# Sending the first 256 tokens ahead, spreading sums of v by engines, two rings of PSUM banks and another sequence, in a long-short attention and feed-forward kernel

## The chip, the core and the metric

The kernel runs on one core of one Trainium2 chip. A core has a matrix engine (TensorE, in profiles PE, with its weight loads as PEld), a vector engine (VectorE, DVE), a scalar engine (ScalarE, ACT), a general engine (GpSimd, POOL) and a sync engine (SyncE, SP), which here issues all DMAs. Each runs its own queue of instructions in order and waits for the others by semaphores. SBUF is the core's working memory with 128 partitions, PSUM the memory that PE writes its products to, in banks. The metric is the device time in microseconds (us); lower is better.

## The reference

Attention over 4 batches, 8 heads, 768 positions and 64 dimensions, with keys near the query and a summary of each block of 32 keys, and then a feed-forward net with softplus:

```python
k_sum = k.reshape(B, H, nb, block, D).max(axis=3)          # block = 32
v_sum = v.reshape(B, H, nb, block, D).mean(axis=3)
scores_l = scale * np.matmul(q, k.transpose(0, 1, 3, 2))
mask_l = np.abs(pos[:, None] - pos[None, :]) < window       # window = 16
scores_s = scale * np.einsum('bhsd,bhnd->bhsn', q, k_sum) + np.log(block)
scores_all = np.concatenate([np.where(mask_l, scores_l, -1e9), scores_s], axis=-1)
a = np.exp(scores_all - max); a = a / (sum(a) + 1e-09)
x = a @ concatenate([v, v_sum])       # then (3072 tokens, 512)
h = x @ w_in                          # 512 x 2048
g = np.maximum(h, 0.0) + np.log1p(np.exp(-np.abs(h)))       # softplus
out = g @ w_out                       # 2048 x 512
```

All is fp32.

## The kernel before

**Precision.** PE's fast 32-bit format keeps fewer bits than fp32, so each large product is made from two parts of each factor: x = xh + xl, w = high + low, and three matmuls, xh·high, xl·high, xh·low. So the weights too must be taken apart on the chip before use.

**Units of work.** The 3072 tokens are 12 chunks of 256. Chunks are handled in groups: [0,1], [2], [3,4], and so on to [11]. The feed-forward net is cut into 16 tiles of d_ff, f = 0 to 15, of 128 each. A step f of group x is written fx.f: a product (`product`, L823, into a bank `ph`), softplus twice on ACT (rounded into `gh`, L843, and exact, in place, L847), the rest `gl` = exact - rounded on DVE (L851), and the matmuls with w_out into banks `po` (L860). The phases are group 0 with f0 to f10, group 1 with f0 to f10, group 0 with f11 to f15, group 1 with f11 to f15, and from group 2 on all 16 steps in one.

**Weights.** Weight tile w0 to w15 (one of w_in and one of w_out, for all 128 of its d_ff) is loaded once (`raw`, L738 and L741) and stays in SBUF. Its chain is: magnitude (DVE L754 or ACT L757), clamp (DVE L761), shift (DVE L765), sign (DVE L769), tail (ACT L775 or DVE L778), the sum of both (`t<-t,raw`, POOL L783), `high` (ACT or DVE, L787) and `low` (DVE or POOL, L794). The work tile `t` comes from a ring of two. w0 and w1 go in two halves of 512 columns, the others in one of 1024.

**Attention** of a chunk goes by pairs of heads, four to a chunk, written ax.i.hp for chunk i of group x: scores on PE (L601), mask and maximum on DVE (L614), exponentials on ACT (L622), their inverse sums on DVE (L629, L630), normalisation on DVE or POOL (L635), a transpose, values on PE (L692, into `xo`), then xh on ACT (L708) and xl on DVE (L712). For group 0 PE transposes (`pt`, L648, copied to `pT` by ACT, L652); for the others DVE transposes blocks (L661) and DMAs through DRAM do the rest. The block sums of keys are a reduction on DVE (L329). Those of v are for the first batch matmuls with ones (`vt`, L407) and a copy by ACT (`vn`, L420), for the others additions on DVE or POOL (L357 to L362). In group 0 the class `FirstPlaces` loads q and v of both chunks at once (L542, L550) and puts the sums of v beside the values by four DMAs that repeat each row for eight windows (`load_sums`, L555).

**Order.** The program is first recorded as some 1600 tasks, each with an engine and in some cases a second one. Then `issue` runs them in the order of a stored list of numbers, `SEQUENCE`; a letter behind a number picks the other engine. So the queue of each engine is fixed by hand before it starts, and a task that isn't ready holds up all that stand behind it in its engine's queue. PSUM banks: two of `ph` (shared with `vt` and later `xo`), one tile of two banks for scores, four of `po` (shared with `pt` and `xo` in group 0).

Of the kernel before, what the change touches and what calls it, by code (L numbers as in the profile page):

```python
# [152 lines left out]
171a 130 109 199 94 172 40 200 110 111 173 41 112 42 174 387 175 239 113 95 197 176 121 114 123 122 115 124 198
177 219 125 220 181a 178 309 209 126 182 185 318 127 201a 183 388 310 184 240 394 202 311 210 186 319 312 408
205 313 249 203 325 187 204 320 592 390 321 188 391 225 279 314 206 322 221a 315 395 316 594 250 317 207a 323
396 208 222 331 223 224 241a 326 397 324 398a 415 399 226 327 245 329 328 400 229 332 242 230 227 330 269 243
389 333 228 337 280 215 392 244 211a 334 246 335 416 338 343 212 213 339 247 214 336 248 344 345 341 417 340 216
574 401 346 393 342 595 347 591 217a 218 348 255 578 418 575 593 419 349 402 403 231a 404 289 235 232 233 355
350 234 579 236 351 352 353 576 356 290 420 357 600a 405 237a 421 270 238 603 406 358 251a 354 407 361 577a 252
580 422 253 367 362 409 254 413 412 604 256 363 425 423 359 368 411 275 424 364 410 257a 369 360 258 605 365  # L160
581a 584 414 373 588 618 259 295 606 370 366 374 585a 371 375 582 426 589 376 299 260 372 427 428 378 377 607
429 381 382a 583 383 435 300 430 431 619 432 380 436 271 437 379 438 433 272 434 273 586 441 620 274 596 617 447
442 608 276 621 443 439 448 444 609 449 265 440 450 453 277a 305 590 278a 459 454 455 456 445 587 384 446 261
451 626a 385 452 460 262 386 461 457 598 285 263 629 264 465 643 462 266 644 630 601 471 466 648a 645 467 610
458 468 472 463 267a 473 631 474 464 291 469 470 268 477 292 483 293 478 632 294 651 475 479 633a 666 484 667
485 476 281a 296 480 481 486 634 489 635 670a 282 482 297 602 498 283 612 490 284 613 665 298 491 487 499 492
286 500 652 488 301a 506 501 287a 653 302 673 288 502 794 597 303 493 797 304 494 796 507 795 512 599 495a 306
793 496a 508 611 497 509 503 654 307 655a 504 518 513 656 308a 514 515 657 674 505 524 532 519 536 802 520 675
521 614 805 636 622 510 637 625 676 638 677a 639 511 624 525 678 623 516 627 806 628 526 615 517 820 821 527 807
# [4 lines left out]
693 694 699 702 834 850 835 851 862 707 855 804 871 836 800 837 700 708 703 705 709 704 710 852a 706 713 856a  # L174
# [40 lines left out]
def kernel(  # L215
# [32 lines left out]
    NU = 4  # L248
# [18 lines left out]
    def bank(shape, name):  # L267
        return buffer(shape, F32, name, "ph", 2, psum, True)
# [255 lines left out]
    class FirstPlaces:  # L524


        def __init__(self, hp, sums, own, sp):
# [4 lines left out]
            def q(g):  # L532
                return own[g]()[:, :n_c * CH]
# [478 lines left out]
```

## Time and profile before

| what | us |
|---|---|
| median of 3 runs | 628.37 (627.63 to 628.79) |
| the profiled execution, its own time | 630.34 |
| its span in the trace | 628.5 |
| PE busy in the span | 611.5 (97%) |
| ACT busy | 311.7 (50%) |
| DVE busy | 277.5 (44%) |
| POOL busy | 83.2 (13%) |

The span is what the trace covers, from the first to the last instruction; the program's time has 1.84 us more around it. PE's busy time counts matmuls; its weight loads lie beside them. In lists of rows "start, duration, engine, line, operation, output<-inputs, shapes" a bracket behind a row tells how long the engine stood idle before it and for whom. In rows of groups the bar separates the count from the busy time, the mean in ns and the idle time before.

### The profile page before, as it was taken

The numbers are of one execution on the slowest core, as the hardware profiler recorded it, in microseconds if no ns is written. First come the engines' busy times: TensorE is split into PE (matmuls) and PEld (weight loads), VectorE is DVE, ScalarE is ACT, GpSimd is POOL, SyncE is SP. The second block draws the span as 40 slices with busy tenths as digits, with TensorE's granted clock in tenths as the row PEclk, the third lists the DMA queues.
The fourth block names the chain that finished last, engine by engine and source line by source line (L and its number), as shares of the span: only waits on it lengthen the run. The fifth ranks groups of instructions, "written<-read, shape, count | busy, mean of one in ns | idle before, by whom it ended". The sixth has DMA issues, their size and how long they took to land.

```text
span 628.5 us, 11315 instructions
## 1 busy us (share of the span) xinstructions
PE 611.5 (97%) x4348; PEld 505.5 (80%) x4348; DVE 277.5 (44%) x757; ACT 311.7 (50%) x752; POOL 83.2 (13%) x74
## 2 busy tenths in 40 slices
PE   4889999999999999999999999999999999999997
PEld 4478888888888888888888888888888888888996
DVE  5978988679644443212451444432411111341111
ACT  1789988479652554316472435462622222553222
POOL 5324341434310202101000030000000000000000
PEclk9799999999999999999999999999999999999999
DMA  8779678933767861241344553543300400311000
GB/s 292 234 244 347 217 190 242 291 92 113 231 199 212 236 181 63 86 139 43 135 152 131 176 141 107 153 144 110 100 0 1 141 0 2 108 66 68 34 1 33
DMA packets 84453, 85.72 MB, mean 136 GB/s; under 512 B 24528, under 2 KB 70192, under 8 KB 84400
## 3 DMA queue, kind: packets, MB, share of 16 engines
q1 hardware_dynamic: 84400, 85.01, 44.0%
q8 instruction: 34, 0.56, 0.4%
q14 instruction: 19, 0.16, 0.1%
HBM read 64.23 MB, written 18.35 MB: 131 GB/s over the span
## 4 chain that ended last, share of the span: by engine, by line
PE 95%; DMA 1%; issue 1%; POOL 1%; SPq 1%; ACT 0%; DVE 0%; POOLq 0%; DVEq 0%
PE po L860 42%; PE ph L823 42%; PE sc L601 4%; PE xo L692 4%; DMA first<-v_hp_dram 1%; PE vt L407 1%; PE warm L934 1%; POOL added L296 0%; SPq L555 0%; PE pt L648 0%; DVE sp L614 0%; ACT sp L622 0%; SPq L738 0%; SPq L741 0%; ACT vn L420 0%
## 5 line engine op out<-in xcount | busy, mean ns | idle before, releaser
L823 PE MATMUL ph<-xh,w 128*128 128x512 f32 (+1 forms) x896 | 257.6, 360 | 0.0
L860 PE MATMUL po<-w,gh 128*128 128x512 f32 x768 | 201.1, 392 | 0.0
L823 PEld LDWEIGHTS ph<-xh,w 128*128 128x128 f32 x896 | 161.7, 189 | 27.2 <-issue 0.5
L851 DVE TENSOR_TENSOR gl<-ph,gh 128x512 fp32r<-128x512 f32 (+1 forms) x112 | 68.1, 611 | 222.4 <-ACT ph L847 203.8
L860 PEld LDWEIGHTS po<-w,gh 128*128 128x128 f32 x768 | 142.1, 188 | 29.5 <-issue 0.5
L823 PE MATMUL ph<-xl,w 128*128 128x512 f32 (+1 forms) x448 | 160.8, 359 | 0.0
L843 ACT ACTIVATE gh<-ph 128x512 fp32r<-128x512 f32 (+1 forms) x112 | 60.2, 537 | 196.0 <-PE ph L823 169.4
L860 PE MATMUL po<-w,gl 128*128 128x512 f32 x384 | 113.7, 393 | 0.0
L823 PEld LDWEIGHTS ph<-xl,w 128*128 128x128 f32 x448 | 84.5, 189 | 13.1
L860 PEld LDWEIGHTS po<-w,gl 128*128 128x128 f32 x384 | 71.0, 188 | 15.5 <-issue 1.0
L622 ACT ACTIVATE sp<-sp,nm 128x120 f32<-128x120 f32 x192 | 73.1, 383 | 2.5 <-DVE nm L614 2.3
L847 ACT ACTIVATE ph<-ph 128x512 f32<-128x512 f32 (+1 forms) x112 | 59.4, 532 | 0.0
L783 POOL TENSOR_TENSOR t<-t,raw 128x1024 int32<-128x1024 int32 (+1 forms) x18 | 43.5, 2421 | 81.7 <-DVE t L769 24.9
L614 DVE CUSTOM_DVE_ANT_0 sp<-sc,added 128x120 f32<-128x120 f32 x192 | 40.7, 278 | 15.2 <-PE sc L601 15.0
L843 ACT ACT_TABLE_LOAD x24 | 30.8, 1283 | 33.5 <-PE ph L823 31.7
L622 ACT ACTIVATION_READ_ACCUMULATOR sp<-sp,nm 128x1 f32 x192 | 36.1, 188 | 0.0
L712 DVE TENSOR_TENSOR xl<-xo,xh 128x512 fp32r<-128x512 f32 x24 | 16.5, 687 | 39.1 <-ACT xh L708 39.1
L708 ACT CAST xh<-xo 128x512 fp32r<-128x512 f32 x24 | 14.1, 590 | 39.2 <-PE xo L692 39.2
L661 DVE STREAM_TRANSPOSE tb<-sp 128x1024 f32<-128x1024 f32 x20 | 24.8, 1240 | 2.3 <-POOL sp L635 2.0
L692 PEld LDWEIGHTS xo<-pT,v 120*64 120x64 f32 x640 | 20.3, 138 | 6.7 <-issue 6.2
L635 POOL TENSOR_TENSOR sp<-sp,ss 128x960 f32<-128x960 f32 x7 | 12.5, 1793 | 98.3 <-DVE ss L630 75.9
L622 ACT ACT_TABLE_LOAD x18 | 23.1, 1283 | 4.8 <-DVE nm L614 4.5
(64 smaller groups left out, 389.7 us busy)
## 6 DMA issues: line engine op xcount, KB each, us to landing
squares<-tb SPq DMA_DIRECT2D x20, 512.0 KB
pT<-squares SPq DMA_DIRECT2D x80, 128.0 KB
raw<-w_in_dram SPq DMA_DIRECT2D x16, 512.0 KB
raw<-w_out_dram SPq DMA_DIRECT2D x16, 512.0 KB
kf<-kT_dram SPq DMA_DIRECT2D x16, 384.0 KB
out_dram<-ob SPq DMA_DIRECT2D x11, 512.0 KB
q<-qT_dram SPq DMA_DIRECT2D x20, 256.0 KB
st<-v_hp_dram SPq DMA_DIRECT2D x12, 384.0 KB
```

Source lines behind the costliest of these rows:

```text
L601: nc.tensor.matmul(unit(g * NU + h * NPAIR + i)[r * QW:(r + 1) * QW, k0:k1], lhsT=q[rows, w * QW:(w + 1) * QW], rhs=k[rows], start=True, s ...
L614: nc.vector.tensor_tensor_reduce(out=sp()[:, n], in0=unit(n), in1=added()[:, kinds.index((lows[w], lows[w + 1]))], scale=-SCALE, scalar=FL ...
L622: nc.scalar.activation(sp()[:, n], sp()[:, n], AF.Exp, bias=nm()[:, n:n + 1], scale=-1.0, accum_out=ss()[:, n:n + 1],)
L661: nc.vector.transpose(out=tb().rearrange("p k (u q) -> p u k q", q=SQ), in_=tiles.sp().rearrange("p u (k q) -> p u k q", q=SQ),)
L692: nc.tensor.matmul(xo()[h * D:(h + 1) * D, g * CH + w * QW:g * CH + (w + 1) * QW], lhsT=tiles.v(g)[:, w, h * D:(h + 1) * D], rhs=queries(g ...
L712: nc.vector.tensor_sub(out=of_x(xl), in0=of_bank(), in1=of_x(xh).bitcast(F32))
L783: nc.gpsimd.tensor_tensor(a, a, word(0, I32), op=ALU.add)
L823: nc.tensor.matmul(ph()[:, :n_x], lhsT=w1()[:, i1, part, cc * P:(cc + 1) * P], rhs=a()[:, cc, :n_x], start=cc == 0 and i == 0, stop=cc == ...
L843: nc.scalar.activation(gh()[:, :n_x], ph()[:, :n_x], AF.Softplus)
L847: nc.scalar.activation(ph()[:, :n_x], ph()[:, :n_x], AF.Softplus)
L851: nc.vector.tensor_sub(out=gl()[:, :n_x], in0=ph()[:, :n_x], in1=gh()[:, :n_x].bitcast(F32),)
L860: nc.tensor.matmul(po[t](), lhsT=a()[:, t * P:(t + 1) * P], rhs=w2()[:, i2, part], start=f == f0 and i == 0, stop=f == f1 - 1 and i == 2,)
```

## The change

Six things change.

1. q and v of group 0 are loaded by chunk and pair of heads (`load_q`, `load_v`), where q and most of v came for both chunks at once. Eight loads of q stand for four, 18 of v for 14.
2. The four DMAs `load_sums` go; eight copies `spread` (24 x 512 elements each) on POOL, DVE or ACT come. The sequence puts five on POOL, one on DVE and two on ACT.
3. Attention of group 0 is declared chunk by chunk, where it was head pair by head pair. Product, softplus, rest and second matmuls of group 0 are made for each chunk of 256 tokens apart in f0, f1 and f2 (`AHEAD = 3`), so that chunk 0 can go through three steps before chunk 1 is there.
4. The ring of four `po` banks becomes two rings of two, `po0` and `po1`, filled in turn by chunk (`half`, `turns`); `pt` takes the ring of its chunk, `xo` of group 0 the second.
5. The copy of `pt` to SBUF and that of xh in group 0 may run on DVE as well.
6. The sequence is another, with other choices of engine. Up to w15: ten magnitudes of 1024 columns more on DVE and ten fewer on ACT, six `low` more on POOL and six fewer on DVE, five `high` fewer on DVE, two tails more on DVE, five normalisations more on POOL and three fewer on DVE.

The diff, cut to its core:

```diff
 SEQUENCE = """
-2 133 43 160 45 64 68 47 1 0 96 134 3 49 4 138a 5 51 135 44 6 7 97 161a 136 8 100 137 9 142 46 10 11 165a 53 12
...
+    def half(h, shape, name):
+        return buffer(shape, F32, name, f"po{h}", 2, psum)
...
-    SPLIT = NF // 2
+    AHEAD = 3
...
     for x, f0, f1 in phases:
+        turns[x, f0] = turn
+        turn = (turn + len(groups[x])) % 2
...
-                def load_q(g=g):
-                    src = qT[0, groups[0][0]:groups[0][-1] + 1, :, hp + g].rearrange("j p c -> p j c")
-                    nc.sync.dma_start(out=q(g).rearrange("p (j c) -> p j c", c=CH), in_=src)
...
-                def load_sums(g=g):
-                    src = sums.first(hp + g).rearrange("n (o c) -> n o c", o=1)
-                    nc.sync.dma_start(out=v(g)[KW:], in_=src.broadcast_to([NB, n_w, P]))
...
+                    def load_q(g=g, i=i, j=j):
+                        nc.sync.dma_start(out=q(g, i), in_=qT[0, j, :, hp + g])
...
+                    def spread(copy, g=g, w0=w0):
+                        src = sums.first(hp + g).rearrange("n (o c) -> n o c", o=1)
+                        copy(out=v(g)[KW:, w0:w0 + NWIN], in_=src.broadcast_to([NB, NWIN, P]))
+                    tiles.v_keys.append((own[g], "sums", i))
+                    order.add(
+                        POOL, pool(NWIN * P), lambda f=spread: f(nc.gpsimd.tensor_copy), [sums.first_v], [tiles.v_keys[-1]],
+                        ways=[
+                            Way(DVE, dve(NWIN * P), lambda f=spread: f(nc.vector.tensor_copy), port=True),
+                            Way(ACT, act(NWIN * P), lambda f=spread: f(nc.scalar.copy)),
+                        ],
+                    )
...
-                pt = buffer([P, NU * P], F32, "pt", "po", NT, psum)
+                pt = half(i, [P, NU * P], "pt")
...
-        xo = buffer([P, NG * CH], F32, "xo", "po", NT, psum) if by_pe else bank([P, NG * CH], "xo")
+        xo = half(1, [P, NG * CH], "xo") if by_pe else bank([P, NG * CH], "xo")
...
-        po = [buffer([P, DM], F32, "po", "po", NT, psum) for _ in range(n_t)]
+        h0 = turns[x, f0]
+        po = [half((h0 + t // 2) % 2, [P, DM], "po") for t in range(n_t)]
...
+            split = x == 0 and f < AHEAD
+            for part in [(i,) for i in range(size)] if split else [tuple(range(size))]:
+                ph = bank([P, CT], "ph")
+                cols = slice(part[0] * CH, (part[-1] + 1) * CH)
...
-        for i, tiles in enumerate(places.tiles):
-            n = hp // NG * len(places.tiles) + i
-            attention(0, i, hp, tiles, T0 - 1.5 - 4.0 * (NHP // NG * len(places.tiles) - 1 - n), True)
+        places.append(FirstPlaces(hp, sums, own, scratch(12 + hp // NG, "sp0")))
+    for i in range(len(groups[0])):
+        for hp in range(0, NHP, NG):
+            attention(0, i, hp, places[hp // NG].tiles[i], T0, True)
```

The new lines of the operations are: magnitude L771, clamp L778, shift L782, sign L786, tail L795 on DVE, POOL's sum L800, `high` L804, `low` L811, rest L876, transpose L675, normalisation L646, spread L564.

**First place: DVE's queue between two rests of group 0, where weight tiles w6 to w9 are made.** Before, between the rests of f2 and f3 (`t_771` is the work tile of w7, `t_832` that of w9; the `gl` are the rests):

```order
L851 TENSOR_TENSOR gl_889<-ph_737,gh_834 128x512
L761 TENSOR_SCALAR t_832<-t_832 128x1024
L765 TENSOR_SCALAR t_832<-t_832 128x1024
L794 TENSOR_TENSOR w_899<-t_771,w_899 128x2x512
L769 SCALAR_TENSOR_TENSOR t_832<-raw_587,t_832 128x1024
L851 TENSOR_TENSOR gl_930<-ph_817,gh_895 128x512
```

And now, between the rests of f3 and f4 (`t_972` is the work tile of w9, `t_990` that of w6, `tb_979` a transposed tile of chunk 2):

```order
L876 TENSOR_TENSOR gl_974<-ph_927,gh_940 128x512
L778 TENSOR_SCALAR t_972<-t_972 128x1024
L675 STREAM_TRANSPOSE tb_979<-sp_389 128x8x4x32
L782 TENSOR_SCALAR t_972<-t_972 128x1024
L786 SCALAR_TENSOR_TENSOR t_972<-raw_863,t_972 128x1024
L778 TENSOR_SCALAR t_990<-t_990 128x1024
L782 TENSOR_SCALAR t_990<-t_990 128x1024
L786 SCALAR_TENSOR_TENSOR t_990<-raw_877,t_990 128x1024
L876 TENSOR_TENSOR gl_1030<-ph_948,gh_977 128x512
```

Between the two rests stood four operations on weights; now there are six and a transpose, and the `low` of w9 stands behind the second rest.

**Second place: POOL's queue at the start, after the constants.** Before (`t<-t,raw` is the sum of a weight tile, `w<-t,w` its `low`):

```order
L783 TENSOR_TENSOR t_152<-t_152,raw_114 128x512
L949 MEMSET sp_222 128x8x8
L783 TENSOR_TENSOR t_136<-t_136,raw_110 128x512
L794 TENSOR_TENSOR w_228<-t_136,w_228 128x512
L794 TENSOR_TENSOR w_290<-t_152,w_290 128x512
L783 TENSOR_TENSOR t_397<-t_397,raw_225 128x512
L783 TENSOR_TENSOR t_327<-t_327,raw_160 128x512
L783 TENSOR_TENSOR t_475<-t_475,raw_292 128x1024
L783 TENSOR_TENSOR t_558<-t_558,raw_469 128x1024
```

And now (`sp0` are exponentials of group 0, `ss` their inverse sums, `vn0` the sums of v, `first` the place of q and v of a pair of heads):

```order
L646 TENSOR_TENSOR sp0_182<-sp0_182,ss_209 128x960
L800 TENSOR_TENSOR t_221<-t_221,raw_203 128x512
L811 TENSOR_TENSOR w_291<-t_221,w_291 128x512
L800 TENSOR_TENSOR t_296<-t_296,raw_271 128x512
L646 TENSOR_TENSOR sp0_279<-sp0_279,ss_301 128x960
L981 MEMSET sp_389 128x8x8
L811 TENSOR_TENSOR w_430<-t_296,w_430 128x512
L800 TENSOR_TENSOR t_352<-t_352,raw_298 128x512
L646 TENSOR_TENSOR sp0_182<-sp0_182,ss_370 128x960
L564 COPY first_141<-vn0_382 24x512
L811 TENSOR_TENSOR w_445<-t_352,w_445 128x512
L800 TENSOR_TENSOR t_434<-t_434,raw_380 128x512
```

Only weights stood there; now three normalisations and a spread stand between them, and all four halves of `low` are on POOL.

More of the change, by code (lines that the diff above doesn't have):

```diff
@@ L153 @@
[L153 to L157, printed above, removed]
@@ L563, in __init__ @@
+                tiles.q = lambda g, i=i: q(g, i)
                 tiles.v = lambda g, w0=w0: v(g)[:, w0:w0 + NWIN]
@@ L649, in attention, with transposed @@
                 order.add(PE, 0.48, transpose, [ident, tiles.sp_key], [pt])
[L651 to L653 removed]
+                def transposed(copy, g=g, pt=pt):
+                    copy(out=pT()[:KS, g * NU * P:(g + 1) * NU * P], in_=pt()[:KS])
+                order.add(
+                    ACT, act(NU * P, True), lambda f=transposed: f(nc.scalar.copy), [pt], [(pT, g)],
+                    ways=[Way(DVE, dve(NU * P), lambda f=transposed: f(nc.vector.tensor_copy))],
+                )
         else:
@@ L705, in of_bank, with high @@
             return xo().rearrange("p (g c) -> p g c", g=NG)
-        def high():
-            nc.scalar.copy(out=of_x(xh), in_=of_bank())
-        order.add(ACT, act(NG * CH, True), high, [xo], [(xh, c, hp)])
+        def high(copy):
+            copy(out=of_x(xh), in_=of_bank())
+        order.add(
+            ACT, act(NG * CH, True), lambda f=high: f(nc.scalar.copy), [xo], [(xh, c, hp)],
+            ways=[Way(DVE, dve(NG * CH), lambda f=high: f(nc.vector.tensor_copy))] if by_pe else [],
+        )
         def low():
@@ L828, in feed_forward @@
-            parts = [range(0, NG), range(NG, NCC)] if x == 0 and f < 2 else [range(NCC)]
-            for ccs in parts:
-                def product_of(ccs=ccs, product=product):
-                    product(ccs)
-                task = order.add(
-                    PE, 0.35 * size * len(ccs), product_of,
-                    [(a, c, hp) for a in (xh, xl) for c in groups[x] for hp in range(0, NHP, NG) if hp in ccs]
-                    + [(w1, i) for i in range(2)],
-                    [ph], due=when, after=[last] if last and ccs[0] == 0 else [],
-                )
-                if ccs[0] == 0:
-                    last = task
@@ L854, in feed_forward @@
-            order.add(DVE, dve(n_x), rest, [ph, gh], [gl])
-            def project(tokens, which, f=f, w2=w2, i2=i2, gh=gh, gl=gl):
-                for t in tokens:
-                    for i, (a, part) in enumerate(((gh, 0), (gh, 1), (gl, 0))):
-                        if (a is gl) in which:
-                            nc.tensor.matmul(
-                                po[t](), lhsT=a()[:, t * P:(t + 1) * P], rhs=w2()[:, i2, part],
-                                start=f == f0 and i == 0, stop=f == f1 - 1 and i == 2,
-                            )
@@ L867, in feed_forward @@
                     order.add(
-                        PE, 0.7, lambda t=t, p=project: p([t], (False, True)), [gh, gl, *parts], [po[t]],
-                        due=then + 0.7 * t,
-                    )
-            else:
-                every = range(n_t)
-                order.add(PE, 0.47 * n_t, lambda p=project: p(every, (False,)), [gh, *parts], po, due=then)
-                order.add(PE, 0.235 * n_t, lambda p=project: p(every, (True,)), [gl, *parts], po, due=then + 0.9 * size)
+                        PE, 0.47 * len(banks), lambda p=project, t=tokens: p(t, (False,)), [g_key[0], *parts], banks,
@@ L876, in feed_forward @@
+                        due=then,
+                    )
+                    order.add(
+                        PE, 0.235 * len(banks), lambda p=project, t=tokens: p(t, (True,)), [g_key[1], *parts], banks,
+                        due=then + 0.9 * size,
+                    )
+        last = lasts[-1]
         products.append(last)
```

199 lines of the change are left out of this document (118 added, 81 removed), and 33 rows, old and new, of the table SEQUENCE.

## The prediction

> **What bounds the kernel now.** I read the page first (span, slices, chain), then the busy time by stretch, then the chain in order of time, then single rows of VectorE (DVE) and GpSimd (POOL). The page:
>
> ```profile
> span 628.5 us, 11315 instructions
> ...
> PE   4889999999999999999999999999999999999997
> ...
> PE 95%; DMA 1%; issue 1%; POOL 1%; SPq 1%; ACT 0%; DVE 0%; POOLq 0%; DVEq 0%
> ```
>
> TensorE (PE) is the chain, and it is full from the third slice on. So the time is PE's work plus whatever PE waits: a wait added anywhere moves the end by its length, and a gain is to be had at the start only. Busy time by stretch (columns: window, length, PE, weight loads, DVE, ACT, POOL, clock, DMA):
>
> ```profile
> 0.00:50.00 50.00, 36.60 (x510) 28.30 (x511) 36.25 (x111) 29.67 (x90) 18.16 (x34) 0.90 0.81 256
> 50.00:164.00 114.00, 114.00 (x840) 95.79 (x839) 95.73 (x213) 91.20 (x183) 44.86 (x20) 1.00 0.69 214
> ```
>
> PE is idle for 13.4 us of the first 50 and never in the next 114. Now the point that I think decides. PE needs weight tile w15 for step f0.15, and POOL makes its last part:
>
> ```profile
> 49.67 4.30 PE ph L823 x18
> ...
> 160.92 2.57 POOL L794 TENSOR_TENSOR w<-t,w 128x1024 fp32r<-128x1024 f32 x1 [1.16 <-ACT w L787]
> ...
> 164.65 2.72 PE ph L823 x12
> ...
> 622.18 2.76 PE po L860 x12
> ```
>
> The tile is done at 163.49 and the product that reads it is running at 164.65 (its step is the one of that row, going by the order of the steps): the weights are prepared just in time, with about 1 us to spare. They are made by DVE, ACT and POOL, and DVE and POOL hinder each other:
>
> ```profile
> 28.77 2.52 POOL L783 TENSOR_TENSOR t<-t,raw 128x512 int32<-128x512 int32 x2 [8.73 <-DVE nm L614]
> 30.08 1.24 DVE L629 TENSOR_SCALAR ss<-ss 128x8 f32<-128x8 f32 x1
> 34.56 0.17 DVE L629 TENSOR_SCALAR ss<-ss 128x8 f32<-128x8 f32 x1 [0.40 <-ACT sp L622]
> 67.29 1.16 DVE L635 TENSOR_TENSOR sp<-sp,ss 128x960 f32<-128x960 f32 x1
> 67.48 3.26 POOL L783 TENSOR_TENSOR t<-t,raw 128x1024 int32<-128x1024 int32 x1 [5.13 <-DVE ss L630]
> 74.51 2.44 POOL L783 TENSOR_TENSOR t<-t,raw 128x1024 int32<-128x1024 int32 x1 [3.77 <-DMA raw<-w_in_dram]
> ```
>
> An 8-element operation takes 0.17 us alone and 1.24 us beside a POOL sum, ending with it (31.32 and 31.29). A POOL sum takes 2.44 us alone and 3.26 us when a two-input DVE operation is under way. So POOL and DVE's work from SBUF to SBUF run one after the other: I call this the lock. DVE's reads of PSUM, its reduction and its transpose I take as free of it, which makes the lock's work smaller. Their groups in 0 to 164 us:
>
> ```profile
> L614 DVE CUSTOM_DVE_ANT_0 sp<-sc,added 128x120 f32<-128x120 f32 x78 | 16.5, 277 | 2.6 <-PE sc L601 2.6
> L851 DVE TENSOR_TENSOR gl<-ph,gh 128x512 fp32r<-128x512 f32 x14 | 9.4, 678 | 2.5 <-ACT ph L847 2.4
> L329 DVE TENSOR_REDUCE ks<-kf 128x24 f32<-128x768 f32 x8 | 7.5, 942 | 1.5 <-DMA kf<-kT_dram 1.5
> L614 DVE DVE_READ_ACCUMULATOR2_ANT nm<- 128x1 f32 x77 | 6.4, 83 | 0.0
> L661 DVE STREAM_TRANSPOSE tb<-sp 128x1024 f32<-128x1024 f32 x5 | 6.2, 1239 | 0.1
> L851 DVE TENSOR_TENSOR gl<-ph,gh 128x256 fp32r<-128x256 f32 x11 | 4.6, 422 | 4.9 <-ACT ph L847 4.8
> L712 DVE TENSOR_TENSOR xl<-xo,xh 128x512 fp32r<-128x512 f32 x6 | 4.1, 685 | 1.6 <-ACT xh L708 1.6
> L895 DVE COPY ob<-po 128x512 f32<-128x512 f32 x3 | 2.0, 686 | 1.0 <-POOL vs L360 1.0
> L630 DVE RECIPROCAL ss<-ss 128x8 f32<-128x8 f32 x9 | 1.8, 203 | 0.3
> ```
>
> They sum to 58.5. DVE is busy 36.25 + 95.73 = 132.0, so at least 73.5 us of it is under the lock; with POOL's 18.16 + 44.86 = 63.0 the lock is held 136.5 of 164 us, a share of 0.83. The rest are moments in which the next holder waits for something else.
>
> **The change part by part.** *Work that changes engine, up to w15.* Counted from the order of both kernels, priced by these rows:
>
> ```profile
> L754 DVE TENSOR_SCALAR t<-raw 128x1024 uint32<-128x1024 uint32 x3 | 2.1, 687 | 0.0
> L794 POOL TENSOR_TENSOR w<-t,w 128x1024 fp32r<-128x1024 f32 x2 | 5.0, 2490 | 2.4 <-DVE vs L369 1.3 <-ACT w L787 1.2
> L794 DVE TENSOR_TENSOR w<-t,w 128x1024 fp32r<-128x1024 f32 x12 | 15.2, 1268 | 0.4 <-ACT w L787 0.2
> L635 POOL TENSOR_TENSOR sp<-sp,ss 128x960 f32<-128x960 f32 x2 | 3.6, 1790 | 2.6 <-DVE ss L630 2.6
> L635 DVE TENSOR_TENSOR sp<-sp,ss 128x960 f32<-128x960 f32 x7 | 8.9, 1277 | 0.2
> L787 DVE CAST w<-t 128x1024 fp32r<-128x1024 f32 x7 | 4.8, 690 | 1.6 <-POOL t L783 1.4
> L794 POOL TENSOR_TENSOR w<-t,w 128x512 fp32r<-128x512 f32 x2 | 2.6, 1278 | 2.6 <-DVE w L787 1.9 <-ACT w L787 0.7
> L761 DVE TENSOR_SCALAR t<-t 128x1024 f32<-128x1024 f32 x14 | 10.4, 745 | 5.9 <-ACT t L757 5.8
> L765 DVE TENSOR_SCALAR t<-t 128x1024 uint32<-128x1024 uint32 x14 | 10.1, 722 | 0.4
> L765 DVE TENSOR_SCALAR t<-t 128x512 uint32<-128x512 uint32 x4 | 1.7, 424 | 0.1
> ```
>
> Ten big magnitudes go from ACT to DVE: 10 x 0.687 = +6.9. Six big `low` go from DVE to POOL: 6 x (2.490 - 1.268) = +7.3. Five big `high` go from DVE to ACT: -5 x 0.69 = -3.4, and two big tails come to DVE: +1.4, at the row of a cast of that size. Five normalisations more on POOL and three fewer on DVE: 5 x 1.79 - 3 x 1.277 = +5.1. The half tiles of w0 and w1 move both ways; I leave them at nothing (two of their `low`, now on POOL, would be +1.2 at most).
>
> *The spreads.* Four DMAs become eight copies, five on POOL, one on DVE, two on ACT. The trace has no POOL copy. Upper bound 1.278 us, a POOL subtraction of as many elements per partition; lower bound 0.424, DVE's one-input row of that size. I take the upper one, since POOL is the slower engine in the pair of L794 rows: 5 x 1.278 + 0.424 = +6.8; by the lower one it is +2.5. Whether such a copy locks at all only a page says: by the Trainium skill, "SBUF — State Buffer", section "Who interferes with whom", a GpSimd instruction that reads SBUF contends with a two-input DVE one, and these copies read it. Without it the forecast would be some 8 us lower.
>
> The lock's work up to w15 becomes 136.5 + 6.9 + 7.3 - 3.4 + 1.4 + 5.1 + 6.8 = 160.6. At a share of 0.83 that takes 193 us: w15 comes 29 us later, and PE, which had 1 us to spare, waits as long, a little at each step on the way. The share is the term's uncertainty. DVE and POOL together are busy 54.4 of the first 50 us and 140.6 of the next 114, 1.09 and 1.23 per us against 1.19 over both; scaled so, the share is 0.76 in the one stretch and 0.86 in the other, and the slip 47 or 22 us. I take 0.83, since the added work lies in both. **+29.**
>
> *Where it shows.* In the first place of the order shown above, DVE has two clamps, two shifts, two signs and a transpose between the rests of f3 and f4: 2 x (0.745 + 0.722 + 1.22) + 1.24 = 6.6 us, and w9's add on POOL (2.44), due in the same stretch under the lock. Before, from the rest of f2 to that of f3:
>
> ```profile
> 69.65 0.65 DVE L851 TENSOR_TENSOR gl<-ph,gh 128x512 fp32r<-128x512 f32 x1
> 74.21 0.68 DVE L851 TENSOR_TENSOR gl<-ph,gh 128x512 fp32r<-128x512 f32 x1
> ```
>
> 4.56 us. PE takes 2.72 + 2.76 = 5.5 us for a step (the rows of 164.65 and 622.18) and needs a rest in each. Before, DVE is ahead of it; after, 7 to 9 us of work stand in a step of 5.5. This is part of the 29, not more.
>
> *Queues.* SP issues four DMAs more (eight loads of q for four, 18 of v for 14, four spreads gone), with the same bytes of q and v. It no longer stands still:
>
> ```profile
> SPq L555 <- ACT sp L622: 9.1, 1, 9.1
> ```
>
> Behind that wait stood the weight loads of the next tile. Bounds: 9.1 us earlier at best, nothing at worst; taken as 0, because in the new order loads of q, k and v for chunk 2 come ahead of those weights. On POOL the spreads and normalisations stand ahead of weight adds (second place of the order): each waits for its exponentials or for the sums of v, and the adds behind it wait too. That lowers the share and is a reason not to take the 0.86.
>
> *First 256 tokens ahead.* Attention of chunk 0 for all heads first, then steps f0 to f2 for its half. A step in halves has 24 matmuls for 12, of half the width: under 0.2 us more per step, three steps, within PE's waits. The first product can start earlier than 49.67, by up to the 9.1 us that SP stood still. I count 0 of it, since what ends the stretch is w15 and not the start. If the weights kept up it would be a gain (rival 1).
>
> *Two rings of two banks instead of one of four.* A group of two chunks uses all four in both, so 0; the ends would be one drained bank per change of group, 2.7 us, or nothing.
>
> *Behind w15.* The attention of the next groups and the sums stand behind the weights in the same queues and come late too. Unknown: from 0 to three waits of the length that the trace shows in 40 to 45 us, 2.73:
>
> ```profile
> 40.00:45.00 5.00, 2.27 (x25) 1.95 (x26) 1.66 (x4) 2.78 (x5) 1.76 (x1) 0.99 1.09 311
> 45.00:50.00 5.00, 4.97 (x70) 4.26 (x67) 4.12 (x5) 4.51 (x7) 2.41 (x1) 0.67 0.86 269
> ```
>
> I take two, **+5.5**. These rows show another cost: after the wait the granted clock is 0.67 for 5 us, 1.65 us of work lost. Four waits of that length cost **+6.6** (0 to 8). Against this stands the Trainium skill, "TensorE: Matmul & The Clock Gate", Part 1: the gate goes to half rate after an idle window of about 3.4 us, by which waits of 2.7 us would cost nothing and the forecast would be 6.6 us lower. The row has a lowered clock after a shorter wait, so I keep the row.
>
> Sum: 29 + 5.5 + 6.6 = +41. The profiled execution took 630.34 us (span 628.5 and 1.84 around it), so 671.4; the median of the runs, 628.37, is 1.97 lower: **669**.
>
> **The rivals.** *1. Faster.* The weights keep up, and the start's gain stays: 628.4 - 9.1, the length of SP's wait, + 0.6 for the halves = 620. This needs w15 by 154 us, so 160.6 us of lock work in less time than it takes: it decides only if POOL and DVE overlap more than the rows above show. Against it are the rows at 30.08 and 67.48; for it, PE's 13.4 idle us at the start.
>
> *2. A draw.* The new order packs the lock almost without gaps: at a share of 0.98, w15 at 164, and the clock and late groups cost 0 to 12: 628 to 640. For it: the share is an outcome of the order, not a limit, and the order is new. Against it: POOL's queue now mixes three chains.
>
> *3. The change doesn't do what it says:* the first product starts no earlier, because spreads and normalisations wait in POOL's queue. Then the time is still w15's, and near 675.
>
> **How the numbers follow.** The forecast (w15 at least 10 us late) has 0.81, rival 1 has 0.07, rival 2 has 0.10, rival 3 has 0.02. About 0.2% is what a measurement of this kernel can tell from no change. Of rival 2, 0.03 lies within it, 0.01 below and 0.06 above. Faster 0.08, same 0.03, slower 0.89. Low end 640: the share of 0.86 gives +22 and the other terms at 0 give 650, and part of what lies between there and the draw belongs to it. High end 694: 0.76 gives +47, with 5.5 and 6.6 688, and with the late groups at three waits and the clock at 8 us 692. Left out are rivals 1 and 2 and 0.03 above.
>
> **What would show it.** Right: PE waits between 45 and 200 us, mostly for DVE's rest and `low`; w15's last row near 190; POOL rows of 3 us and more; the clock under 1.00 in several slices; after that PE full again. Wrong: PE without waits from 50 us on, or POOL's and DVE's SBUF rows overlapping at their lone durations. The forecast fails most easily if the spreads are cheap and the share comes out near 0.95.

## The result and the profile after

| | before | after |
|---|---|---|
| median, us | 628.11 (627.63 to 628.79) | 665.39 (662.84 to 666.82) |
| span of the profiled execution, us | 628.5 | 664.8 |
| first product starts, us | 49.60 | 41.73 |
| last `low` of a weight tile (w15) ends, us | 163.49 | 190.18 |
| PE busy / idle in the span, us | 611.5 / 17.0 | 623.8 / 41.0 |

The ratio is 1.059 (95% interval 1.055 to 1.063): slower by 5.9%. The page of the changed kernel, the lines that answer to those of before (tenths in 40 slices of 16.6 us):

```profile
span 664.8 us, 11397 instructions
...
PE   8688779997979989999999999999999999999997
...
DVE  5989999888964443253434341441111220111211
...
PEclk9988999997979989999999999999999999999999
...
PE 71%; DVE 15%; DMA 5%; SPq 3%; issue 3%; ACT 3%; POOL 0%; DVEq 0%; POOLq 0%; ACTq 0%
```

PE's slices under nine tenths now reach to 249 us, where before only the first three, up to 47 us, and the last were so low, and DVE has a share of 15% in the chain that ended last, where it had none. Before, no wait of PE ended with a rest; now these do (total, times, longest):

```profile
PE ph L845 <- DVE gl L876: 12.3, 5, 4.9
PE po L883 <- DVE gl L876: 8.0, 5, 2.6
```

Both are waits for a rest, a 0.4 to 0.7 us operation that stands in DVE's queue behind work on weights. The longest of them, read in DVE's rows and the row of PE that ends it:

```profile
181.73 1.22 DVE L786 SCALAR_TENSOR_TENSOR t<-raw,t 128x1024 uint32<-128x1024 uint32 x1
182.87 0.16 DVE L640 TENSOR_SCALAR ss<-ss 128x8 f32<-128x8 f32 x1
...
183.31 3.12 DVE L646 TENSOR_TENSOR sp<-sp,ss 128x960 f32<-128x960 f32 x1
186.47 1.25 DVE L675 STREAM_TRANSPOSE tb<-sp 128x1024 f32<-128x1024 f32 x1
187.63 0.65 DVE L876 TENSOR_TENSOR gl<-ph,gh 128x512 fp32r<-128x512 f32 x1
...
188.97 1.21 DVE L811 TENSOR_TENSOR w<-t,w 128x1024 fp32r<-128x1024 f32 x1
```

```profile
183.03 2.38 POOL L800 TENSOR_TENSOR t<-t,raw 128x1024 int32<-128x1024 int32 x1 [3.35 <-DVE ss L640]
```

```profile
188.34 0.80 PE L845 MATMUL ph<-xh,w 128*128 128x512 f32 x1 [4.94 <-DVE gl L876]
```

The normalisation takes 3.12 us where 1.28 was its mean before. POOL's sum holds the lock from 183.03 to 185.41; from there to 186.43 is 1.02 us. The rest comes behind it, and PE stands idle for 4.94 us before its next product. The last row of DVE, the `low` of w15, ends at 190.18.

What the lock does is seen best in the means of DVE's groups (0 to 200 us, after):

```profile
L786 DVE SCALAR_TENSOR_TENSOR t<-raw,t 128x1024 uint32<-128x1024 uint32 x14 | 22.7, 1624 | 0.4
...
L778 DVE TENSOR_SCALAR t<-t 128x1024 f32<-128x1024 f32 x14 | 17.2, 1231 | 0.3
L771 DVE TENSOR_SCALAR t<-raw 128x1024 uint32<-128x1024 uint32 x13 | 17.0, 1304 | 0.2
L782 DVE TENSOR_SCALAR t<-t 128x1024 uint32<-128x1024 uint32 x14 | 15.1, 1081 | 0.3
L811 DVE TENSOR_TENSOR w<-t,w 128x1024 fp32r<-128x1024 f32 x6 | 11.2, 1863 | 0.1
...
L646 DVE TENSOR_TENSOR sp<-sp,ss 128x960 f32<-128x960 f32 x3 | 5.4, 1811 | 0.1
```

The same operations on the same shapes had means of 1221, 745, 687, 722, 1268 and 1277 ns before; the row of the first of them, of before:

```profile
L769 DVE SCALAR_TENSOR_TENSOR t<-raw,t 128x1024 uint32<-128x1024 uint32 x14 | 17.1, 1221 | 0.4
```

The rise times the counts is 5.6 + 6.8 + 8.0 + 5.0 + 3.6 + 1.6 = 31 us that DVE spends inside its instructions waiting for POOL. Row by row, with the half tiles and against the lone times, it is 40 us: 18 beside POOL's sums, 14 beside its `low`, 7 beside its normalisations and under 1 beside its copies; none of the long rows is without a row of POOL beside it. Such a row counts as busy: DVE reads "49.45 of 50" in the row of 50 to 100 us and yet does less.

```profile
50.00:100.00 50.00, 41.18 (x210) 32.09 (x209) 49.45 (x58) 26.47 (x47) 26.50 (x10) 0.93 0.54 175
```

### The profile page after: what moved, and what is told of

It is laid out like the page before. It is cut to its first block, busy times and chain, and to the rows that moved or that the text cites. A ratio compares the mean times of both kernels' runs of the same rounds, so it can differ in the third digit from the quotient of the medians.

```text
span 664.8 us, 11397 instructions
## 1 busy us (share of the span) xinstructions
PE 623.8 (94%) x4384; PEld 514.3 (77%) x4384; DVE 312.3 (47%) x755; ACT 293.9 (44%) x741; POOL 122.2 (18%) x98
## 4 chain that ended last, share of the span: by engine, by line
PE 71%; DVE 15%; DMA 5%; SPq 3%; issue 3%; ACT 3%; POOL 0%; DVEq 0%; POOLq 0%; ACTq 0%
PE ph L845 33%; PE po L883 31%; PE xo L706 4%; DVE t L782 2%; PE sc L612 2%; DVE t L778 2%; DVE w L811 1%; ACT sp L633 1%; DVE t L786 1%; DVE t L771 1%; PE warm L965 1%; DVE gl L876 1%; DMA raw<-w_out_dram 1%; DMA squares<-tb 1%; DMA ob<-part 1%
## 5 line engine op out<-in xcount | busy, mean ns | idle before, releaser
L845 PE MATMUL ph<-xh,w 128*128 128x512 f32 (+1 forms) x920 | 264.8, 362 | 13.6 <-DVE gl L876 12.3
L883 PE MATMUL po<-w,gh 128*128 128x512 f32 x768 | 203.9, 395 | 0.2 <-DVE ob L922 0.2
L845 PEld LDWEIGHTS ph<-xh,w 128*128 128x128 f32 x920 | 168.5, 193 | 43.2 <-DVE gl L876 15.0
L876 DVE TENSOR_TENSOR gl<-ph,gh 128x512 fp32r<-128x512 f32 (+1 forms) x115 | 67.9, 597 | 221.9 <-ACT ph L872 217.2
L845 PE MATMUL ph<-xl,w 128*128 128x512 f32 (+1 forms) x460 | 165.5, 360 | 0.0
L883 PE MATMUL po<-w,gl 128*128 128x512 f32 x384 | 115.5, 397 | 8.0 <-DVE gl L876 8.0
L845 PEld LDWEIGHTS ph<-xl,w 128*128 128x128 f32 x460 | 89.0, 193 | 13.4 <-DVE xl L729 0.3
L646 POOL TENSOR_TENSOR sp<-sp,ss 128x960 f32<-128x960 f32 x15 | 28.1, 1873 | 257.6 <-DVE ss L641 235.7
L800 POOL TENSOR_TENSOR t<-t,raw 128x1024 int32<-128x1024 int32 (+1 forms) x18 | 41.1, 2281 | 51.3 <-DVE t L786 23.5
L633 ACT ACT_TABLE_LOAD x20 | 25.7, 1283 | 12.3 <-DVE nm L625 11.3
L811 POOL TENSOR_TENSOR w<-t,w 128x1024 fp32r<-128x1024 f32 (+1 forms) x12 | 27.4, 2280 | 18.3 <-ACT w L804 11.2
L722 ACT CAST xh<-xo 128x512 fp32r<-128x512 f32 x22 | 12.8, 581 | 37.4 <-PE xo L706 37.4
L675 DVE STREAM_TRANSPOSE tb<-sp 128x1024 f32<-128x1024 f32 x20 | 24.8, 1239 | 9.6 <-DMA squares<-tb 6.1
```

Source lines behind the costliest of these rows:

```text
L633: nc.scalar.activation(sp()[:, n], sp()[:, n], AF.Exp, bias=nm()[:, n:n + 1], scale=-1.0, accum_out=ss()[:, n:n + 1],)
L646: engine.tensor_tensor(sp(), sp(), s, op=ALU.mult)
L675: nc.vector.transpose(out=tb().rearrange("p k (u q) -> p u k q", q=SQ), in_=tiles.sp().rearrange("p u (k q) -> p u k q", q=SQ),)
L800: nc.gpsimd.tensor_tensor(a, a, word(0, I32), op=ALU.add)
L811: engine.tensor_tensor(part(1, F32R), rows(t), part(0, F32), op=ALU.subtract)
L845: nc.tensor.matmul(ph()[:, :n], lhsT=w1()[:, i1, low, cc * P:(cc + 1) * P], rhs=a()[:, cc, cols], start=cc == 0 and i == 0, stop=cc == NCC ...
```

## The experiments

All are one of the two kernels with one thing changed. Ratios are to the kernel before as it was measured again beside each series, with medians of 628.1 to 630.3 us. "w15" is the end of the last `low` in the profile, "lock" the union of POOL's rows and DVE's rows that work from SBUF to SBUF up to there, "share" lock over w15.

| kernel | lock | w15 | share | span | span - w15 | median |
|---|---|---|---|---|---|---|
| before | 136.8 | 163.5 | 0.84 | 628.5 | 465.0 | 628.1 |
| changed | 154.4 | 190.2 | 0.81 | 664.8 | 474.6 | 665.4 |
| old_order_new_engines | 149.6 | 178.3 | 0.84 | 643.1 | 464.8 | 644.6 |
| new_order_old_engines | 142.0 | 212.2 | 0.67 | 688.2 | 476.1 | 689.9 |
| code_with_old_order | 136.7 | 172.7 | 0.79 | 637.8 | 465.1 | 639.9 |
| old_code_with_new_order | 151.0 | 200.9 | 0.75 | 672.0 | 471.1 | 674.7 |
| new_start | 148.4 | 174.5 | 0.85 | 639.6 | 465.1 | 641.5 |
| short_adds | 122.1 | 164.6 | 0.74 | 633.4 | 468.8 | 635.1 |
| memset_adds | 145.1 | 174.2 | 0.83 | 642.1 | 467.9 | 646.1 |
| split_adds | 155.0 | 183.6 | 0.84 | 655.1 | 471.5 | 656.0 |
| magnitudes_on_act | 149.3 | 203.5 | 0.73 | 674.9 | 471.4 | 677.5 |
| lows_on_dve | 147.4 | 186.9 | 0.79 | 660.9 | 474.0 | 662.5 |
| spreads_on_act | 151.4 | 189.9 | 0.80 | 660.8 | 470.9 | 664.0 |
| retuned_old | 135.4 | 183.2 | 0.74 | 649.9 | 466.7 | 649.7 |

The sixth column is the main finding. While w15 moves over 49 us, what comes behind it takes 464.8 to 466.7 us in the five kernels that have the old order behind w15 (retuned_old with small moves), and 467.9 to 476.1 in the others. So the end of the last weight tile tells the time of these kernels to about 1%. It is a mark, and it isn't shown that PE waits for the tile itself: in the changed kernel 20.3 us of PE's waits end with a rest and 0.2 us with a part of a weight tile (`w`, L811). Rests and weights stand in the same queue of DVE, so both come late together.

**Which part of the change?** First the code without the order, then the order without the code.

```diff
# code_with_old_order: the changed code; the sequence puts its tasks as the kernel before had them
-0 43 3 4 5 6 7 8 9 10 11 12 13 44 45 68 14 15 16 64 17 18 47 46 92 49 82 78 2 93 48 19 20 21 1 50 145 22 23 24
...
+2 145 43 172 45 64 72 68 75 47 1 0 78 86 146 3 49 4 150a 5 51 147 44 6 7 79 87 173a 148 8 82 89 90 149 9 154 46 10
...
```

> The changed code (loads by chunk, spreads, halves of f0 to f2, two rings) with the order and the engine choices of the kernel before; halves stand where the whole steps stood, spreads are on ACT where the four DMAs stood. Theory L (time follows the work under the lock between POOL and DVE): that work is back at 136.5 us, so 628 to 634 us. Theory O (the order of the queues decides): 628 to 638. Theory C (the parts of the code cost it): near 660.

Measured 639.85 (ratio to before 1.016, interval 1.014 to 1.019). A little over the ranges of L and O, and far from C's 660. Its first product is at 55.07, 5.5 us later than before, since the halves and spreads stand only roughly where they should; w15 comes at 172.7, and the rest is as before.

```diff
# old_code_with_new_order: the code of before; the sequence puts its tasks as the changed kernel has them
-2 133 43 160 45 64 68 47 1 0 96 134 3 49 4 138a 5 51 135 44 6 7 97 161a 136 8 100 137 9 142 46 10 11 165a 53 12
+0 43 3 4 5 6 7 8 9 10 11 12 13 44 45 68 14 15 16 64 17 18 47 46 72 49 100 96 2 73 48 19 20 21 1 50 133 22 23 24 25
...
```

> The code of the kernel before (whole steps, four DMAs for the sums of v, one ring) with the order and the engine choices of the changed kernel; a whole step stands where its second half stood. L and O: 655 to 675 us, as the changed kernel or a little more. C: 628 to 635.

Measured 674.74 (1.072, interval 1.069 to 1.075). The loss comes with the sequence; C is out. Halves, spreads and rings are a matter of 10 us at the rough places that they have here: with the old order +10 (ratio 1.016), with the new one -8 (1.059 with them, 1.072 without).

**Engines or order?** The sequence holds both: numbers set the order, letters the engine.

```diff
# old_order_new_engines: in the sequence of before, 51 letters as in the changed kernel
-2 133 43 160 45 64 68 47 1 0 96 134 3 49 4 138a 5 51 135 44 6 7 97 161a 136 8 100 137 9 142 46 10 11 165a 53 12
+2 133 43 160 45 64 68 47 1 0 96 134a 3 49 4 138 5 51 135 44 6 7 97 161a 136 8 100 137 9 142 46 10 11 165 53 12
...
```

> Code and order of the kernel before; only the choices of engine for magnitude, high, low, tail and normalisation are those of the changed kernel. L: lock work 136.5 + 6.9 + 7.3 - 3.4 + 1.4 + 5.1 = 153.8 us, at a share of 0.83 185 us, w15 21 us later, with a few us of lowered clock 649 to 655 us. O: an order made for other engines loses something, under 640. C: 628.

Measured 644.55 (1.024, interval 1.021 to 1.026), between the ranges of O and L, and in neither. L had the direction: the lock's work rose, though by 12.8 us and not 17.3, the share stayed at 0.84, and so w15 came 14.8 us later. The engines alone cost 14 us in the old order (before took 630.34 in this series).

```diff
# new_order_old_engines: in the sequence of the changed kernel, the same 51 letters back
-25 94 95 96 146a 26 27 28 147 29 30 31 104 32 33 34 97 163 148 149 150 151 51 105 55 72 152a 168 75 53 164a 154
+25 94 95 96a 146 26 27 28 147 29 30 31 104 32 33 34 97 163 148 149 150a 151 51 105 55 72 152 168 75 53 164a 154
...
```

> Code and order of the changed kernel; the choices of engine for magnitude, high, low, tail and normalisation are those of the kernel before (spreads as in the changed kernel). L: lock work 136.5 + 6.8 = 143.3 us, at 0.83 172 us, so 8 us of slip are left: 636 to 646 us. O: the order keeps its loss or loses more, 660 to 690.

Measured 689.88 (1.096, interval 1.093 to 1.099), some 24 us worse than the changed kernel and at the upper end of O's range. L failed: the lock's work fell as it said (142.0, forecast 143.3), but the share fell to 0.67. So the letters that cost 14 us in the old order save 24 in the new one. The waits of DVE in this kernel, 40 to 212 us:

```profile
DVE t L778 <- ACT t L774: 23.6, 9, 7.0
DVE w L811 <- ACT w L804: 7.3, 3, 3.4
```

DVE's clamp is the next thing in its queue and waits for a magnitude that now stands deep in ACT's (before, the same wait came to 5.8 us in 4 times). One part each, to see how far the sum's terms hold in the new order:

```diff
# magnitudes_on_act: 11 letters of the changed sequence, ten of large tiles
-162a 178 182 80 84 622 418 37 438 67a 425 101 38 201 202 39 102a 103 140 142 73 40 141 76 109 111 130 183 41 74
+162a 178 182 80 84 622 418 37 438 67a 425 101 38 201 202 39 102a 103 140 142 73 40 141 76 109 111 130 183a 41 74
...
# lows_on_dve: 10 letters
-170a 171a 177 173a 65 66 159a 100 70 60 62 158 160 161 35 119 120 129 36 63 81 85b 83 79 71b 174 424 175 176 181
+170a 171 177 173a 65 66 159a 100 70 60 62 158 160 161 35 119 120 129 36 63 81 85b 83 79 71b 174 424 175 176 181
...
# spreads_on_act: 6 letters
-170a 171a 177 173a 65 66 159a 100 70 60 62 158 160 161 35 119 120 129 36 63 81 85b 83 79 71b 174 424 175 176 181
+170a 171a 177 173a 65 66 159a 100 70 60 62 158 160 161 35 119 120 129 36 63 81b 85b 83 79 71b 174 424 175 176 181
...
```

> The changed kernel with the magnitudes of the weight tiles back on the engines of the kernel before (ten large ones from DVE to ACT). The prediction's sum: -6.9 us of lock, at 0.81 -8.5: 655 to 659 us. Theory that an order fits its own engines: a clamp on DVE then waits for ACT's queue (as in new_order_old_engines, 23.6 us in 9 waits), 670 to 685.

> The changed kernel with the lows of the weight tiles back on the engines of the kernel before (six large ones net and two small ones from POOL to DVE). The prediction's sum: -7.3 us, at 0.81 -9: 655 to 658 us. Theory that an order fits its own engines: the lows take DVE's time ahead of the rests that PE waits for, 661 to 668.

> The changed kernel with all eight spreads on ACT. The prediction's sum gave the spreads 6.8 us of lock (five at 1.278 us on POOL, one at 0.424 on DVE); by the rows measured it is 3.4 + 0.42 = 3.8, at a share of 0.81 4.7 us: 659 to 662 us. If eight copies on ACT delay what stands behind them there: 665 or more.

Measured 677.51, 662.46 and 664.02: the first two in the ranges of the theory that an order fits its own engines, the third between its two ranges. The lock's work did fall, by 5.1, 7.0 and 3.0 us (forecast 6.9, 7.3 and 3.8), but the time didn't follow. The magnitudes are +12 us where the sum gives -8.5, with this wait in DVE's queue:

```profile
DVE t L778 <- ACT t L774: 29.4, 8, 7.3
```

The lows are -3 where the sum gives -9, and the spreads -1.4 where it gives -4.7, less than these runs tell apart. So in the new order none of these three terms, taken back singly, gives its price in time.

**Is it the lock?** Two kernels make POOL's sums harmless in two ways.

```diff
# short_adds: a sixteenth of the columns; the tails of the others are left out
-                nc.gpsimd.tensor_tensor(a, a, word(0, I32), op=ALU.add)
+                m = a.shape[-1] // 16
+                nc.gpsimd.tensor_tensor(a[:, :m], a[:, :m], word(0, I32)[:, :m], op=ALU.add)
```

> The changed kernel, but POOL's sums of the weight tiles (L800) are made over the first sixteenth of the columns only, so the tails of the other columns are left out; order and engines are as in it. POOL's 18 sums took 35.7 + 5.4 = 41 us. Lock theory: DVE loses 31 us inside its own instructions to POOL (the rise of its means at L771, L778, L782, L786, L811 and L646 times their counts), of which these sums are near half of POOL's tensor work; 640 to 651 us, and the mean of the clamps (L778, 1.23 us) falls towards 0.75. Theory that the order of the queues alone costs the time, without the lock: each tile is ready 2.3 us sooner and no more, 658 to 665 us, clamps as they were.

Measured 635.06 (ratio to before 1.010, interval 1.008 to 1.012): 30 us back, more than was expected. The clamp's mean is 782 ns (1231 in the changed kernel). It doesn't tell the lock from POOL's own queue, which is shorter too. This one does:

```diff
# memset_adds: the same time on POOL, but nothing is read; weights are zeros
-                nc.gpsimd.tensor_tensor(a, a, word(0, I32), op=ALU.add)
+                m = a.shape[-1]
+                nc.gpsimd.memset(a, 0)
+                nc.gpsimd.memset(a[:, :m * 3 // 4], 0)
+                nc.gpsimd.memset(a[:, :m * 3 // 4], 0)
```

> The changed kernel, but each of POOL's sums of the weight tiles (L800) is replaced by three memsets of the same tile with about the same time together (by the rows of memsets 0.95 + 0.74 + 0.74 us for a large one), which read nothing; the weights come out as zeros. If POOL holds the lock with any instruction: 662 to 668 us. If only its reads hinder DVE's two-input instructions (L786, L811, L646) and its writes hinder the others: these had 10.8 of the 31 us lost, near half of it to the sums, so 655 to 662 us, and L786 falls below 1.45 us. If POOL's time matters only by its own queue: 664 to 667 us and all means unchanged.

Measured 646.14, 19 us less than the changed kernel and below all three ranges. DVE's groups there, 0 to 200 us:

```profile
L786 DVE SCALAR_TENSOR_TENSOR t<-raw,t 128x1024 uint32<-128x1024 uint32 x14 | 24.3, 1734 | 0.4
L782 DVE TENSOR_SCALAR t<-t 128x1024 uint32<-128x1024 uint32 x14 | 16.1, 1151 | 0.3
L778 DVE TENSOR_SCALAR t<-t 128x1024 f32<-128x1024 f32 x14 | 13.2, 943 | 0.3
...
L814 DVE TENSOR_TENSOR w<-t,w 128x1024 fp32r<-128x1024 f32 x6 | 7.3, 1218 | 0.8 <-ACT w L807 0.7
L646 DVE TENSOR_TENSOR sp<-sp,ss 128x960 f32<-128x960 f32 x5 | 5.9, 1171 | 0.1
```

```profile
L801 POOL MEMSET t<- 128x1024 int32 x14 | 14.8, 1057 | 30.7 <-DVE t L786 24.1 <-DMA k<-kT_dram 6.6
...
L803 POOL MEMSET t<- 128x768 int32 x14 | 13.8, 984 | 0.8
L802 POOL MEMSET t<- 128x768 int32 x14 | 13.4, 956 | 0.8
```

POOL spends 14.8 + 13.8 + 13.4 = 42.0 us on those of the 14 large tiles, where the sums took 35.7, so its queue is no shorter than before. The two-input operations L814 and L646 are back at their lone times; L786, forecast under 1450 ns, isn't. Single rows tell why, first DVE's, then POOL's:

```profile
43.87 1.41 DVE L778 TENSOR_SCALAR t<-t 128x1024 f32<-128x1024 f32 x1
...
48.48 1.21 DVE L814 TENSOR_TENSOR w<-t,w 128x1024 fp32r<-128x1024 f32 x1
...
52.97 3.31 DVE L786 SCALAR_TENSOR_TENSOR t<-raw,t 128x1024 uint32<-128x1024 uint32 x1
```

```profile
43.30 1.44 POOL L801 MEMSET t<- 128x1024 int32 x1 [1.14 <-DVE t L786]
...
48.49 0.95 POOL L801 MEMSET t<- 128x1024 int32 x1
...
52.62 2.58 POOL L814 TENSOR_TENSOR w<-t,w 128x1024 fp32r<-128x1024 f32 x1 [1.16 <-ACT w L807]
```

Beside a memset the clamp, with one input, takes 1.41 us (0.69 alone), while DVE's `low`, with two, keeps its 1.21. The sign L786 is long beside POOL's `low`, which reads and was left as it was. Four of its 14 large rows are over 2.6 us here, each beside a `low` or a normalisation on POOL; the other ten take 1.21 to 1.23, three of them beside memsets. In the changed kernel three of 14 are long, and none of them beside a sum. So the forecast for L786 laid to the sums what they hadn't cost.

Each sum is also three short instructions here, so that DVE might get in between. The control:

```diff
# split_adds: the sums as three pieces, with all their reads
-                nc.gpsimd.tensor_tensor(a, a, word(0, I32), op=ALU.add)
+                m = a.shape[-1]
+                for c in (slice(0, m * 3 // 8), slice(m * 3 // 8, m * 11 // 16), slice(m * 11 // 16, m)):
+                    nc.gpsimd.tensor_tensor(a[:, c], a[:, c], word(0, I32)[:, c], op=ALU.add)
```

> The changed kernel, each of POOL's sums of the weight tiles cut into three pieces by columns (3/8, 5/16, 5/16), with the same reads, writes and total. It is the control to memset_adds (646.14), whose memsets were also three to a tile. If reads are what counts there: 662 to 670 us, as the changed kernel or a little more for three instructions. If it was the finer grain, which lets DVE in between the pieces: 640 to 652 us.

Measured 656.00 (ratio to before 1.043, interval 1.041 to 1.046), between the two ranges: side by side, 9 of the 19 us came from the finer grain. The means of the clamp, the magnitude and DVE's `low` are 958, 1017 and 1396 ns there, for 1231, 1304 and 1863 in the changed kernel. POOL's pieces of the 14 large tiles take 52.5 us where the whole sums took 35.7, and the kernel is faster all the same: this speaks for the lock and against POOL's own queue. The other 10 came with the memsets. How much of that comes from not reading isn't shown, since the memsets of a large tile are also shorter, 2.42 us alone against 2.73 for the three pieces, and their zeros change PE's data too.

**Where in the order?**

```diff
# new_start: the first 300 numbers of the changed sequence, up to 253 in these lines, then the order and the letters of before
-233 242 301 419 358 625 334 218 219 347 361 362 348 359 367 363 234 235 428 227 236 238 220 239 240a 253 364 254
...
+347 361 362 348 359 367 363 234 235 428 227 236 238 220 239 240a 253 261 291 624 262 429 360 430 254 281 255 292 256
...
```

> The changed code with its own order and engines for the first 300 tasks (up to the rest of f0.3: attention of group 0, halves of f0 to f2, weights to about w7), and the order and engines of the kernel before for the other 1323. Theory that the new start costs the time: 655 to 665 us. Theory that the loss comes behind it, where w8 to w15 are made beside attention of groups 1 and 2: 633 to 645 us, as the changed code with the old order (639.85) or a little less, and the first product starts at the time of the changed kernel.

Measured 641.54 (1.020, interval 1.019 to 1.022), in the range of the theory that the loss comes behind the start. Its first product, and the last `low`:

```profile
42.11 0.36 PE L843 MATMUL ph<-xh,w 128*128 128x256 f32 x1
```

```profile
171.93 2.56 POOL L809 TENSOR_TENSOR w<-t,w 128x1024 fp32r<-128x1024 f32 x1 [1.16 <-ACT w L802]
```

The new start is real, 13 us sooner than in code_with_old_order (55.07), and worth nothing: w15 is 1.8 us later and the time the same. The other 24 us of the loss come behind that point of the sequence, where most of w8 to w15 is made.

**A better version?** One attempt, from the side that the sum pointed to.

```diff
# retuned_old: the sequence of before after many small moves; 24 letters differ
-2 133 43 160 45 64 68 47 1 0 96 134 3 49 4 138a 5 51 135 44 6 7 97 161a 136 8 100 137 9 142 46 10 11 165a 53 12
+132 0 3 4 5 6 43 45 44 46 133 134 135 136 137 160 161a 162 163 164 165 64 68 72 7 8 2 73 100 101 47 69 49 48 96 65
...
```

> The code of the kernel before with a sequence derived from its own by small moves, and fewer lock operations before w15: casts of w0, w1, w8, w12 and w13 from DVE to ACT (-0.42 x 3 - 0.69 x 3 = -3.3 us), tails of w0 and w1 to ACT (-0.9), of w13, w14 and w15 to DVE (+2.1), the low of w15 from POOL to DVE (-1.2): -3.3 us; PE's first transposes stand ahead of others. Lock theory with the share held: w15 some 4 us sooner and 622 to 626 us; if PE is full from 50 us on whatever the weights do, only the start can gain: 624 to 630.

Measured 649.71 (1.034, interval 1.032 to 1.037): both theories missed. PE's waits there:

```profile
PE sc L598 <- DMA first<-qT_dram: 6.5, 1, 6.5
...
PE sc L598 <- DMA q<-qT_dram: 4.2, 1, 4.2
```

The lock's work did fall (135.4), but loads moved within SP's queue and PE waited for q, and the share went to 0.74. No kernel here beats the one before.

## Why the prediction was right, and where it was not

The time was forecast at 669 and is 665.4. Point by point:

- *w15 sets the time.* Right as a mark: the column span - w15, with w15 forecast at 193 and found at 190.2. Of the waits the account was half right. PE was to wait 29 + 5.5 us more, mostly for rests and `low`; it stood idle for 24.0 us more (17 up to w15, 7 behind it), hardly for `low`, and was busy for 12.3 us longer.
- *The lock's work up to w15.* Forecast 160.6, by the union of rows 154.4. The spreads were mis-sized: 695 ns each on POOL, not 1278, which with the one on DVE is 3.8 us for the 6.8. The normalisations on DVE up to w15 fell by four, from seven to three, and not by three: 1.3 us less. The last 2 us aren't accounted for. That a copy holds the lock at all is seen in the changed kernel at 48.04, where a shift on DVE takes 0.99 us, for 0.69 alone, beside a copy on POOL that runs from 47.51 to 48.48.

```profile
L564 POOL COPY first<-vn 24x512 f32<-24x512 f32 x5 | 3.4, 695 | 0.3
```

- *The share of 0.83.* It is 0.81, so the forecast came out. But the step was weaker than it looked, and that it came out was in part luck. It held in kernels whose order was made for their engines (0.84, 0.81) and in the old order with foreign engines (0.84), and failed in the new order with foreign engines (0.67). The prediction took the share as a property of the stretch; it is one of the order and the engines together. Nor can the 37 us be divided between the two: the engines alone cost 14 us in the old order, the new order with the old engines 60 (with the changed code), and both together 37. The errors in work and share also cancelled in part: 154.4 at 0.83 would have put w15 at 186.
- *The first place.* Right: 20.3 us of PE's waits end with a rest. They lie between 47 and 188 us, not at f3 and f4 alone.
- *First 256 tokens ahead, counted as 0.* Right: 8 us sooner (41.73 against 49.60), and in new_start nothing of such a start arrives at the end.
- *Behind w15, and the clock: 5.5 + 6.6 = 12.1.* Measured 474.6 - 465.0 = 9.6 for what comes behind w15, with 7 us more of idle time in it. The clock was mis-sized: over the span it was 0.977 against 0.992 before, and 0.023 x 664.8 = 15.3 us lost against 0.008 x 628.5 = 5.0 make 10 and not 6.6; 3.7 of it lie behind w15, the rest is in w15's 26.7 us already. Four waits, and the rows of the stretches in or behind them:

```profile
49.41 0.50 PE L883 MATMUL po<-w,gl 128*128 128x512 f32 x1 [2.44 <-DVE gl L876]
...
80.22 0.50 PE L845 MATMUL ph<-xh,w 128*128 128x512 f32 x1 [2.10 <-DVE gl L876]
90.16 1.20 PE L883 MATMUL po<-w,gl 128*128 128x512 f32 x4 [2.59 <-DVE gl L876]
...
154.00 0.58 PE L845 MATMUL ph<-xh,w 128*128 128x256 f32 x1 [3.59 <-DVE gl L876]
```

```profile
50.00:55.00 5.00, 4.46 (x43) 3.19 (x41) 4.93 (x5) 2.45 (x3) 3.13 (x2) 0.66 0.80 271
...
80.00:85.00 5.00, 4.79 (x14) 3.82 (x15) 4.96 (x6) 3.82 (x5) 2.94 (x2) 0.66 0.44 142
...
90.00:95.00 5.00, 4.22 (x17) 3.20 (x18) 4.96 (x5) 1.06 (x1) 2.06 (x1) 1.00 0.15 29
...
155.00:160.00 5.00, 5.00 (x24) 4.90 (x23) 2.34 (x2) 0.86 (x3) 1.09 (x1) 0.50 0.00 0
```

Waits of 2.44 and 2.10 us were followed by a clock of 0.66, the one of 2.59 by 1.00, the one of 3.59 by 0.50. The Trainium skill, "TensorE: Matmul & The Clock Gate", Part 1, puts the drop at an idle window of about 3.4 us that runs freely, not from the start of the wait. The row of 50 to 55 doesn't agree with 3.4 us as a least length of a wait. With 3.4 us as that length, the sum, 6.6 us lower, would have been 663. A window that runs freely is in the trace: the granted clock falls to a half and rises again only at moments that are whole multiples of 3.41 us apart (50.81, 54.22, 81.53, 84.94, 153.21, 160.04 and so on). Cut into windows at these moments, PE is idle for 1.9 to 3.4 us in the six windows at full clock that a fall follows, and for at most 1.8 in the others at full clock. The wait of 2.59 us lies across two windows, with 0.8 us in one and 1.8 in the other, and no fall follows. One window at half clock costs 1.7 us of work; the changed kernel has nine, the one before three.

- *The rule on the lock.* The Trainium skill, "SBUF — State Buffer", "Who interferes with whom", lets two-input operations contend with POOL's reads only. The `low` and the normalisation agree: 1863 to 1218 ns and 1811 to 1171 ns between the changed kernel and memset_adds.
- *Rival 1* needed POOL and DVE to overlap; the 31 us inside DVE's instructions are the answer. *Rival 2* needed a share of 0.98; none of the fourteen kernels has more than 0.85. *Rival 3* is out by the first product at 41.73.

## What to carry to other kernels

Look for a mark that tells the time, here the end of the last weight tile, which told that of fourteen kernels to about 1%; then read which waits it stands for, here waits for rests in the same queue. Work that moves from an engine with a lock partner to the partner is not moved off: price both sides, and an order that was made for its engines can lose with others, as both did here (14 and 24 us). A start that is sooner is worth nothing when something else ends the stretch.

## What the runs showed that was not expected

Cutting POOL's sums into three pieces, with more instructions and the same work, made the kernel 9 us faster (665.4 to 656.0): the lock is held for one instruction, so long ones cost the waiting engine more. And a "busy" engine can be a waiting one: DVE's 14 clamps went from 745 to 1231 ns on the same data, and nothing in the busy shares says why.
